# Moving four 20-byte tiles in a fused attention and feed-forward kernel, so that every large tile starts at another byte of SBUF

## The chip, the cores and the metric

The kernel runs on one core of a Trainium2 chip. The metric is the device time of one execution in microseconds (us), lower is better. Times of a kernel are given as the median of several runs; a profile is one more execution with the hardware profiler on.

## The reference

For 8 batches of 8 heads (sequence 576, head dimension 64) the program computes attention with a mask in blocks of 64, and passes the joined heads, as 4608 tokens of width 512, through a feed-forward layer with a hidden width of 2048. All in float32.

```
scores = scale * np.matmul(q, k.transpose(0, 1, 3, 2))
mask = block_i >= block_j                       # blocks of 64
scores = np.where(mask, scores, -1000000000.0)
scores = scores - np.max(scores, axis=-1, keepdims=True)
attn = np.exp(scores)
attn = attn / (np.sum(attn, axis=-1, keepdims=True) + 1e-09)
attn_out = np.matmul(attn, v)
...
x = attn_out.transpose(0, 2, 1, 3).reshape(B * S, H * D)
h = x @ w_in
g = np.maximum(0.01 * h, h)
return (g @ w_out)
```

## The kernel before

**Number format.** Where float32 products are wanted at the rate of one pass, a value is held as two tiles of type float32r, a rounded upper part and the rest: `wih` and `wil` for w_in, `woh` and `wol` for w_out, `xh` and `xl` for the tokens, `gh` and `gl` for the hidden values, `qs`, `kh`, `kl`, `vs`, `pth`, `ptl` in the attention. A product is three matmuls: upper by upper, upper by rest, rest by upper.

**Stages.** At the start the weights come in by pieces through `raw` and `val` and are split into the four weight tiles, while TensorE (PE) works at the attention of the first heads. After that each head (56 of them in the split format, `kind == "full"`) runs scores (L487), a row maximum on VectorE (DVE, `nm`, L505), the exponential on ScalarE (ACT, L514), reciprocals (`rec`, L528 and L529), normalising on whichever of GpSimd (POOL), DVE and ACT is free (L542 to L544), a transposition through DVE and a DRAM tile (`turn`, `way`, `ptm`), the product with v (L641) and the placing into `xr`, which holds one batch of tokens. Of tiles with two buffers, head i uses number i % 2: `qs0`/`qs1`, `kh0`/`kh1`, `kl0`/`kl1`, `nm0`/`nm1`, `rec0`/`rec1`.

**Feed-forward.** Tokens are taken in 18 chunks of 256. For each chunk and each of 8 pairs of hidden tiles, L805 runs two times 12 matmuls of 256 columns (weights `wih`/`wil` loaded, `xh`/`xl` streamed) into `p_h`; ACT makes `g` (L812), a cast makes `gh` (L243), a subtraction makes `gl` (L253 on DVE or L254 on POOL), and L824 runs two times 6 matmuls of 512 columns (`gh`/`gl` loaded, `woh`/`wol` streamed) into `p_o`. In all that is 3456 matmuls at L805 and 1728 at L824. The feed-forward matmuls of one batch are spread between the heads of later ones; the last chunks run alone at the end.

**Order.** The class `Plan` simulates the engines with fixed costs, once, when the program is built, and writes every engine's instructions in the order that it finds. It knows nothing of addresses, so the order doesn't depend on where a tile lies.

**Addresses.** All tiles named here come from one pool, `const`, by the helper `fixed`, and lie in a partition of SBUF one behind the other in the order in which `fixed` is called, each rounded up to 32 bytes. The first 384 bytes are taken by the program itself. A tile `nm0` of 5 float32 values so takes 32 bytes, and the pairs `nm`, `sums` and `rec` take 64 bytes each. All the large tiles have sizes that are multiples of 256 bytes, and most of 512, so that the position of one within a line of 512 bytes is handed on to those behind it. Tiles of the later pools (`raw`, `val`, `xr1`, `ptl`, `ptm`, `turn`, `v_stage` and others) begin behind the last tile of `const`.

Of the kernel before, what the change touches and what calls it, by code (L numbers as in the profile page):

```python
# [9 lines left out]
F32 = mybir.dt.float32  # L10
# [7 lines left out]
P = 128  # L18
# [3 lines left out]
NT = 5  # L22
# [204 lines left out]
def attention_ffn(ctx: ExitStack, tc: tile.TileContext, qk: bass.AP, v: bass.AP, w_in: bass.AP, w_out: bass.AP, out: bass.AP):  # L227
# [33 lines left out]
    def fixed(shape, dt, name, n=None, pool=const):  # L261
        if n is None:
            return pool.tile(shape, dt, name=name)
        return [pool.tile(shape, dt, name=f"{name}{i}") for i in range(n)]
# [3 lines left out]
    def identity(pool):  # L268
        one = fixed([P, P], F32, "ident", None, pool)
        make_identity(nc, one)  # L270
        return one

    wih = fixed([P, ND, DFF], F32R, "wih")
    wil = fixed([P, ND, DFF], F32R, "wil")
    woh = fixed([P, NF, DM], F32R, "woh")
# [24 lines left out]
    kh = fixed([P, S], F32R, "kh", 2)  # L300
    kl = fixed([P, S], F32R, "kl", 2)
    vs = fixed([P, NT, 2 * D], F32R, "vs")
    nm = fixed([P, NT], F32, "nm", 2)
    sums = fixed([P, NT], F32, "sums", 2)
    rec = fixed([P, NT], F32, "rec", 2)
    for y in range(2):
        nc.gpsimd.memset(sums[y], 1.0)
    xr = [fixed([P, ND, S], F32, "xr0"), None]
# [10 lines left out]
    xh = fixed([P, ND, CH], F32R, "xh")  # L319
    xl = fixed([P, ND, CH], F32R, "xl")  # L320
    ob = fixed([P, DM], F32, "ob")

    stage = ExitStack()
    pool = stage.enter_context(tc.tile_pool(name="wst", bufs=1, reuse_waits="tile"))
# [587 lines left out]
```

## Time and profile before

| | us |
|---|---|
| three runs: lowest, median, highest | 1120.43, 1120.84, 1126.4 |
| the profiled execution | 1119.52 |
| its span, first to last instruction | 1117.7 |
| PE busy | 1083.7 (97%) |
| DVE busy | 762.2 (68%) |
| ACT busy | 708.3 (63%) |
| POOL busy | 475.5 (43%) |

Instructions are named by the line of the kernel that issued them; L243, L244, L246, L253 and L254 belong to helpers (`copying`, `subtracting`) and stand for many tiles. PE's matmuls are pipelined: the duration of one contains some 0.16 us in which the next already streams, so that the distance between two starts tells what a matmul costs, and its duration doesn't. PEld is the loading of weights, which runs beside the matmul before.

### The profile page before, as it was taken

How to read it: one execution, taken by the hardware profiler on the slowest of the kernel's cores; microseconds unless marked ns; L12 is line 12 of the kernel's file. 1: busy time of each engine (PE TensorE's matmuls, PEld its weight loads, DVE VectorE, ACT ScalarE, POOL GpSimd, SP SyncE). 2: the span in 40 equal slices, each digit the busy share in tenths (PEclk: the TensorE clock that was granted, in tenths of full speed). 3: DMA queues.
4: the chain of work that ended last, by engine and by line, in shares of the span. 5: the costliest groups of instructions: out<-in, count | busy, mean ns of one | idle time of the engine just before them, and what ended most of it. 6: DMA issues, size and time to landing. Idle time of an engine off the chain costs nothing.

```text
span 1117.7 us, 20595 instructions
## 1 busy us (share of the span) xinstructions
PE 1083.7 (97%) x6896; PEld 971.3 (87%) x6896; DVE 762.2 (68%) x2115; ACT 708.3 (63%) x1696; POOL 475.5 (43%) x501
## 2 busy tenths in 40 slices
PE   5799999999999999999999999999999999999998
PEld 4578788888889989999999998999989998999997
DVE  6998978879878777877666678787877776400000
ACT  7998767767777766655655566676677765322222
POOL 3444244545544444433443345455444445422221
PEclk9999999999999999999999999999999999999999
DMA  7766421157766656564445456656676655200000
GB/s 235 231 201 198 133 95 61 61 173 208 199 198 189 201 170 201 176 170 147 128 151 148 128 171 185 203 171 203 176 205 185 194 156 160 59 20 19 1 20 19
DMA packets 96810, 166.24 MB, mean 149 GB/s; under 512 B 10176, under 2 KB 79808, under 8 KB 96704
## 3 DMA queue, kind: packets, MB, share of 16 engines
q1 hardware_dynamic: 96704, 164.93, 50.0%
q8 instruction: 54, 0.88, 0.3%
q14 instruction: 52, 0.43, 0.1%
HBM read 111.41 MB, written 53.48 MB: 148 GB/s over the span
## 4 chain that ended last, share of the span: by engine, by line
PE 69%; DVE 16%; ACT 6%; DMA 4%; issue 2%; SPq 1%; POOL 0%; ACTq 0%; DVEq 0%; POOLq 0%
PE p_h L805 27%; PE p_o L824 27%; PE p_t L641 6%; PE p_s L487 6%; DVE nm L505 4%; ACT prow L514 4%; DVE turn L703 2%; DVE qs L464 2%; DMA way<-turn 2%; DMA ptm<-way 2%; PE p_t L568 2%; PE p_s L481 1%; DVE p_s L498 1%; DVE ptl L253 1%; SPq L720 1%
## 5 line engine op out<-in xcount | busy, mean ns | idle before, releaser
L805 PE MATMUL p_h<-xh,wih 128*128 128x256 f32 x1152 | 327.0, 284 | 1.6 <-DVE xh L244 1.6
L805 PE MATMUL p_h<-xl,wih 128*128 128x256 f32 x1152 | 323.1, 280 | 1.0 <-DVE xl L253 0.9
L805 PE MATMUL p_h<-xh,wil 128*128 128x256 f32 x1152 | 322.5, 280 | 0.0
L254 POOL TENSOR_TENSOR gl<-g,gh 128x512 fp32r<-128x512 f32 x110 | 149.4, 1359 | 368.2 <-ACT gh L243 317.7
L805 PEld LDWEIGHTS p_h<-xl,wih 128*128 128x128 f32 x1152 | 218.6, 190 | 11.6 <-DVE xl L253 1.4
L805 PEld LDWEIGHTS p_h<-xh,wih 128*128 128x128 f32 x1152 | 217.9, 189 | 11.8 <-DVE xh L244 1.8
L805 PEld LDWEIGHTS p_h<-xh,wil 128*128 128x128 f32 x1152 | 219.4, 190 | 0.0
L514 ACT ACTIVATE prow<-p_s,nm 128x192 f32<-128x192 f32 (+4 forms) x308 | 160.0, 525 | 74.1 <-DVE nm L505 73.4
L812 ACT ACTIVATE g<-p_h 128x512 f32<-128x512 f32 x144 | 86.0, 597 | 174.6 <-PE p_h L805 168.4
L824 PE MATMUL p_o<-woh,gh 128*128 128x512 f32 x576 | 183.1, 399 | 0.0
L824 PE MATMUL p_o<-wol,gh 128*128 128x512 f32 x576 | 179.7, 393 | 0.0
L824 PE MATMUL p_o<-woh,gl 128*128 128x512 f32 x576 | 179.1, 392 | 0.0
L703 DVE STREAM_TRANSPOSE turn<-prow 128x384 f32<-128x384 f32 (+3 forms) x384 | 143.9, 401 | 33.2 <-POOL prow L542 24.0
L542 POOL TENSOR_SCALAR prow<-prow,rec 128x320 f32<-128x320 f32 (+4 forms) x142 | 77.3, 557 | 148.7 <-DVE rec L529 106.7
L505 DVE TENSOR_REDUCE nm<-p_s 128x1 f32<-128x192 f32 (+4 forms) x308 | 137.4, 480 | 3.3
L824 PEld LDWEIGHTS p_o<-woh,gl 128*128 128x128 f32 x576 | 108.2, 188 | 24.8
L824 PEld LDWEIGHTS p_o<-wol,gh 128*128 128x128 f32 x576 | 108.2, 188 | 24.4
L544 ACT ACTIVATE prow<-prow,rec 128x192 f32<-128x192 f32 (+4 forms) x124 | 75.5, 614 | 48.6 <-DVE rec L529 48.4
L243 ACT CAST gh<-g 128x512 fp32r<-128x512 f32 x139 | 86.1, 620 | 22.0 <-PE p_o L824 20.5
L254 POOL TENSOR_TENSOR ptl<-ptm,pth 128x448 fp32r<-128x448 f32 x83 | 97.6, 1193 | 3.6 <-ACT pth L243 3.6
L243 ACT CAST pth<-ptm 128x448 fp32r<-128x448 f32 x191 | 94.4, 564 | 5.4 <-DMA ptm<-way 4.9
L824 PEld LDWEIGHTS p_o<-woh,gh 128*128 128x128 f32 x576 | 90.9, 188 | 3.6 <-issue 0.4
(81 smaller groups left out, 1655.0 us busy)
## 6 DMA issues: line engine op xcount, KB each, us to landing
way<-turn SPq DMA_DIRECT2D x192, 224.0 KB, 3.0
ptm<-way SPq DMA_DIRECT2D x192, 224.0 KB, 4.3
qk_in<-in_qk SPq DMA_DIRECT2D x56, 576.0 KB, 3.8
v_stage<-in_v SPq DMA_DIRECT2D x56, 160.0 KB, 2.3
out<-ob SPq DMA_DIRECT2D x35, 256.0 KB, 2.5
raw<-in_w_in SPq DMA_DIRECT2D x32, 256.0 KB, 3.3
raw<-in_w_out SPq DMA_DIRECT2D x32, 256.0 KB, 3.4
qk_in<-in_qk SPq DMA_DIRECT2D x8, 320.0 KB, 3.6
```

The source lines that it names most:

```text
L243: one = lambda: nc.scalar.copy(dst(), src())
L254: ("POOL", pool2(n), lambda: nc.gpsimd.tensor_sub(dst(), one(), two())),
L487: go = lambda ap=ap, cols=cols, kk=kk, k0=k0, k1=k1, first=first, last=last: nc.tensor.matmul(ap, qs[z][:, cols], kk[:, k0:k1], start=firs ...
L505: [("DVE", dve(kw[t]), lambda t=t, ap=ap, flat=flat: nc.vector.tensor_reduce(nm[z][: qn[t], t : t + 1], ap[: qn[t]], axis=AX.X if flat els ...
L514: nc.scalar.activation(o, ap[: qn[t]], AF.Exp, bias=nm[z][: qn[t], t : t + 1], scale=1.0, accum_out=sums[z][: qn[t], t : t + 1])
L542: ("POOL", pool1(kw[t]), lambda: nc.gpsimd.tensor_scalar(p(), p(), by, 1.0, op0=ALU.mult, op1=ALU.mult)),
L544: ("ACT", act(kw[t], True), lambda: nc.scalar.mul(p(), p(), by)),
L641: nc.tensor.matmul(to, vs[:, j, :], src, start=start, stop=stop)
L703: nc.vector.transpose(dst, src.rearrange("p (s b i) -> p s b i", b=4, i=32))
L805: nc.tensor.matmul(hh[:, i, :], w[:, d, f * P : (f + 1) * P], x[:, d, :], start=k == 0, stop=k == len(terms) - 1)
L812: add([("ACT", act(512), lambda: nc.scalar.activation(g, hh, AF.Prelu, alpha=0.01))], rank, [("h", z)], ["g"])
L824: nc.tensor.matmul(p_o[m], a[:, i, m * P : (m + 1) * P], w[:, 2 * u + i, :], start=u == 0 and k == 0, stop=u == NU - 1 and k == 5,)
```

## The change

The two maxima tiles `nm` are allocated first in the pool, ahead of the weights, and the two reciprocal tiles `rec` last, behind the output buffer `ob`. Nothing else is edited, and the list of instructions, their order on every engine and the semaphores that they wait for are the same in both programs. What differs are start addresses in SBUF:

| tiles, in the order of the pool | before: byte in the partition, and in its 512-byte line | after |
|---|---|---|
| `wih` | 384, 384 | 448, 448 |
| `wil`, `woh`, `wol`, `pth`, `prow0_*`, `qk_in0` | at 384 of a line | at 448 |
| `qs0`, `kh0`, `kl0`, `vs` | at 384 | at 448 |
| `qs1`, `kh1`, `kl1` | at 128 | at 192 |
| `nm0`, `nm1` | 167296, 167328 | 384, 416 |
| `sums0`, `sums1` | 167360, 167392 | the same |
| `rec0`, `rec1` | 167424, 167456 | 197120, 197152 |
| `xr0`, `g`, `gh0`, `gh1`, `gl0`, `gl1`, `xh`, `xl`, `ob` | at 64 | at 0 |
| all later pools | at 64 or 320 | the same |

So the tiles from the weights to `vs` move up by 64 bytes, those from `xr0` to `ob` move down by 64, and between a weight tile of the feed-forward and the activations that it meets the distance grows by 128 bytes. No address in PSUM and none of the DRAM tiles changes.

```
@@ -270,6 +270,7 @@
         make_identity(nc, one)
         return one
 
+    nm = fixed([P, NT], F32, "nm", 2)
     wih = fixed([P, ND, DFF], F32R, "wih")
     wil = fixed([P, ND, DFF], F32R, "wil")
     woh = fixed([P, NF, DM], F32R, "woh")
@@ -300,9 +301,7 @@
     kh = fixed([P, S], F32R, "kh", 2)
     kl = fixed([P, S], F32R, "kl", 2)
     vs = fixed([P, NT, 2 * D], F32R, "vs")
-    nm = fixed([P, NT], F32, "nm", 2)
     sums = fixed([P, NT], F32, "sums", 2)
-    rec = fixed([P, NT], F32, "rec", 2)
     for y in range(2):
         nc.gpsimd.memset(sums[y], 1.0)
     xr = [fixed([P, ND, S], F32, "xr0"), None]
@@ -319,6 +318,7 @@
     xh = fixed([P, ND, CH], F32R, "xh")
     xl = fixed([P, ND, CH], F32R, "xl")
     ob = fixed([P, DM], F32, "ob")
+    rec = fixed([P, NT], F32, "rec", 2)
 
     stage = ExitStack()
     pool = stage.enter_context(tc.tile_pool(name="wst", bufs=1, reuse_waits="tile"))
```

More of the change, by code (lines that the diff above doesn't have):

```diff
@@ L271, in identity @@
         return one
+    nm = fixed([P, NT], F32, "nm", 2)
     wih = fixed([P, ND, DFF], F32R, "wih")
@@ L302, in attention_ffn @@
     vs = fixed([P, NT, 2 * D], F32R, "vs")
-    nm = fixed([P, NT], F32, "nm", 2)
     sums = fixed([P, NT], F32, "sums", 2)
-    rec = fixed([P, NT], F32, "rec", 2)
     for y in range(2):
@@ L321, in attention_ffn @@
     ob = fixed([P, DM], F32, "ob")
+    rec = fixed([P, NT], F32, "rec", 2)
     stage = ExitStack()
```

## The prediction

> **What bounds the kernel now.** I read the table of windows first, cut where the kind of work changes, then PE's own list of waits, then the chain of work that ended last.
>
> The windows of the whole core:
>
> ```profile
> core 0: us, PE busy (x) PEld busy (x) DVE busy (x) ACT busy (x) POOL busy (x), PEclk, DMA share, GB/s
> 0.00:120.00 120.00, 100.87 (x562) 78.38 (x563) 103.61 (x334) 103.48 (x295) 48.32 (x73) 1.00 0.70 214
> 120.00:300.00 180.00, 170.34 (x1094) 151.72 (x1093) 151.59 (x401) 130.23 (x327) 88.28 (x103) 0.98 0.42 126
> 300.00:976.00 676.00, 674.60 (x4357) 616.39 (x4356) 501.11 (x1373) 440.24 (x1019) 306.58 (x301) 1.00 0.59 171
> 976.00:1117.70 141.70, 137.94 (x889) 124.82 (x887) 5.88 (x10) 34.31 (x57) 32.32 (x25) 1.00 0.04 16
> ```
>
> From 300 us PE is busy 674.60 of 676 us, and in the last stretch until its final matmul: 72% of the span belongs to PE alone. DVE has 501 us there and ACT 440, so they may be late without PE noticing. PE's waits in 300:1117 confirm it; the list has one row:
>
> ```profile
> PE p_s L487 <- ACT prow L514: 1.6, 6, 0.4
> ```
>
> Before 300 us the limits are mixed: no engine is full, and the first piece of the chain is a load. So the question is almost only what a matmul at L805 or L824 costs, since these are three quarters of PE's rows. The chain shows that, by the length of unbroken runs (start, length, what):
>
> ```profile
> 470.06 4.16 PE p_o L824 x18
> 476.12 4.24 PE p_h L805 x36
> 753.15 5.65 PE p_h L805 x48
> 978.85 5.46 PE p_h L805 x48
> 1018.80 2.75 PE p_o L824 x12
> 1107.07 6.88 PE p_o L824 x30
> ```
>
> The reader should see two speeds of one and the same work, both at a granted clock of 1.00: 48 matmuls at L805 took 5.65 us (117.7 ns each) at 753 us and 5.46 us (113.75 ns each) at 979 us. L824 has 229.2 and 229.3 ns in the last two rows, 231.1 in the first. No wait stands inside these runs. The two speeds even alternate within a few rows; starts of 12 matmuls at L805 in the last stage:
>
> ```profile
> 1042.06 0.28 PE L805 MATMUL p_h<-xh,wih 128*128 128x256 f32 x1
> 1042.18 0.28 PE L805 MATMUL p_h<-xl,wih 128*128 128x256 f32 x1
> ...
> 1042.65 0.28 PE L805 MATMUL p_h<-xh,wil 128*128 128x256 f32 x1
> 1042.77 0.28 PE L805 MATMUL p_h<-xh,wih 128*128 128x256 f32 x1
> ...
> 1043.45 0.62 PE L824 MATMUL p_o<-woh,gh 128*128 128x512 f32 x2
> ```
>
> Five take 0.59 us (118 ns each), the next seven 0.80 us (114 ns). Something that the profile doesn't name makes a matmul 4 ns dearer for some rows and then lets go. This is the only place where an address could act on the time, and it's what my uncertainty hangs on.
>
> **The change part by part.** It adds, removes and reorders no instruction on any engine, and no wait differs. The four moved tiles are 20 bytes each; `nm` and `rec` are read and written by the same instructions as before. So there is no term for an operation; there are only durations that might depend on a start address. I look for each kind of user at rows of this trace in which the address already differs and all else is equal.
>
> *ACT and DVE.* Even heads use `kh0` and `qs0` (byte 384 of a 512-byte line), odd heads `kh1` and `qs1` (byte 128). ACT's cast for one odd head (window 580:600) and for the even head before it (560:580):
>
> ```profile
> L243 ACT CAST kh<-qk_in 128x576 fp32r<-128x576 f32 x1 | 0.7, 665 | 0.0
> ...
> L243 ACT CAST kh<-qk_in 128x576 fp32r<-128x576 f32 x1 | 0.7, 663 | 0.0
> ```
>
> 665 against 663 ns. A shift of 256 bytes is worth 2 ns, and a shift of 64 bytes has no reason to be worth more. With the 1700 rows at ACT and 2100 at DVE that the windows count, 2 ns each would be 3.4 and 4.2 us of busy time, nearly all under PE's cover after 300 us; uncovered, in the first 300 us with some 620 and 735 rows, it would be at most 1.5 us. I take 0.
>
> *PE in the attention.* L628 streams `ptf` (byte 64) while it loads `vf0` (byte 64) for even heads and `vf1` (byte 320) for odd ones, so that the distance between what is loaded and what is streamed differs by 256 bytes. The odd head at 87.6 us and the even one at 98.0 us:
>
> ```profile
> L628 PE MATMUL p_t<-ptf,vf 128*64 128x256 f32 x6 | 1.5, 388 | 0.0
> L628 PE MATMUL p_t<-ptf,vf 128*64 128x64 f32 x2 | 0.3, 220 | 0.0
> ...
> L628 PE MATMUL p_t<-ptf,vf 128*64 128x256 f32 x6 | 1.5, 388 | 0.0
> L628 PE MATMUL p_t<-ptf,vf 128*64 128x64 f32 x2 | 0.3, 220 | 0.0
> ```
>
> The rows are the same to the nanosecond. L487, which has the split format of the feed-forward, loads `qs` and streams `kh`; an even head (window 687.0:688.2, both tiles at 384) and an odd one (702.1:703.3, both at 128):
>
> ```profile
> L487 PE MATMUL p_s<-kh,qs 128*128 128x320 f32 x1 | 0.4, 391 | 0.0
> L487 PE MATMUL p_s<-kh,qs 128*128 128x448 f32 x1 | 0.4, 362 | 0.0
> ...
> L487 PE MATMUL p_s<-kh,qs 128*128 128x320 f32 x1 | 0.4, 389 | 0.0
> L487 PE MATMUL p_s<-kh,qs 128*128 128x448 f32 x1 | 0.4, 363 | 0.0
> ```
>
> 753 against 752 ns for the two. I take 0 for all matmuls of the attention.
>
> *PE in the feed-forward.* Here the trace has one placement only: activations at 64, weights at 384. The nearest rows are those above, which say 0. They don't cover one thing: a long run of equal matmuls in which loading and streaming repeat at a fixed distance, where the 4 ns appear. The bounds are the two speeds themselves, and I work them out under the rivals. I take 0.
>
> *DMAs.* Destinations or sources that move are `qk_in0` (576 KB at each of 56 heads), `ob`, and `g` for the last store. Their rows:
>
> ```profile
> qk_in<-in_qk SPq DMA_DIRECT2D x56, 576.0 KB, 3.8
> out<-ob SPq DMA_DIRECT2D x35, 256.0 KB, 2.5
> out<-g SPq DMA_DIRECT2D x1, 256.0 KB, 2.0
> ...
> 3.20 5.71 DMA qk_in<-in_qk
> ```
>
> No engine waits for `qk_in` behind 300 us, and `ob` is drained under matmuls. Uncovered are only the opening load, 5.71 us on the chain, and the last store, 2.0 us. If each changed by a tenth it would be 0.6 and 0.2 us; I take 0. The Trainium skill (DMA: Bandwidth & Descriptors, "How a descriptor splits into AXI transactions") says that a piece that doesn't start at a multiple of 256 bytes begins at the boundary below and pays for the bytes ahead. By it a row of the last store (2048 bytes, from byte 64 to byte 0) falls from 9 transactions to 8, an estimate of 0.2 us less, and a row of `qk_in0` keeps its number; no run shows it so far.
>
> **The sum:** 0 on every term, so 1119.5 us, the profiled execution's own time (span 1117.7 and 1.8 around it). That lies 1.3 us under the median of the runs, 1120.84, whose highest is 1126.4.
>
> The page that speaks most plainly here is SBUF — State Buffer of the Trainium skill ("Who interferes with whom"): contention comes only from the port pair that VectorE and GpSimd share, and "PE and ACT never wait on anyone." By it the sum is 0 too. But by it the two speeds of L805 should not exist either, and they do (117.7 and 113.75 ns); so I don't let that rule shut out the next two cases.
>
> **The rivals.**
>
> *A, the feed-forward matmuls all run at the higher speed.* Mechanism: loading and streaming read SBUF at once, 128 bytes further apart than before, and no longer hinder each other. For it: the slow rows come and go in the same place of each unit, with nothing waited for. Against: L628 and L487 show nothing of the kind. Price: in the last stage the chain is L805 for 50.8% of 131 us, which is 115.5 ns for each of 576:
>
> ```profile
> by line: PE p_h L805 50.8%; PE p_o L824 49.2%; PE p_t L641 0.1%
> 976.00:1107.00 131.00, 73.38 (x576) 72.81 (x576) 1.00 0.03 13
> 300.00:976.00 676.00, 294.52 (x2280) 291.20 (x2280) 1.00 0.59 171
> ...
> L805 PE MATMUL p_h<-xl,wih 128*128 128x256 f32 x192 | 53.4, 278 | 0.0
> ...
> L805 PE MATMUL p_h<-xl,wih 128*128 128x256 f32 x760 | 212.2, 279 | 0.0
> ```
>
> The last two rows are one of the three forms of L805 in the last stage (278 ns) and in 300:976 (279 ns); over the three the mean rises by 1.3 ns, so 116.8 ns for 2280. At 113.75 throughout that is 2280 x 3.05 + 576 x 1.75 = 8.0 us less. L824 from the 231.1 of the row at 470 us to the 229.2 of the one at 1019 us, for its 1141 in the middle: 2.2 us less. Together 10.2 us: **1109**.
>
> *B, they all run at the lower speed.* The same place, the other sign: the new distance makes loading and streaming meet in every row. L805 at 117.7: 2280 x 0.9 + 576 x 2.2 = 3.3 us more. For L824 the slowest pairs of the trace give 235 ns (two in 0.47 us):
>
> ```profile
> 500.24 0.63 PE L824 MATMUL p_o<-woh,gh 128*128 128x512 f32 x2
> 500.71 0.63 PE L824 MATMUL p_o<-wol,gh 128*128 128x512 f32 x2
> ```
>
> That is 1141 x 3.8 + 312 x 5.8 = 6.1 us more. Together 9.4 us: **1129**. It decides once L805's long runs in the middle are all at 117 ns and L824 leaves 231; from some 6 us (0.5%) on it can be told from no change.
>
> *C, the addresses don't move as said.* In the built programs they do; no chance.
>
> **How the numbers follow.** No change 0.43, A 0.34, B 0.23. A gets more than B since most of the long runs are at the lower speed now and so have further to fall than to rise. A measurement of this kernel tells about 0.5%, 5.6 us, from no change; the case of no change has 1114 to 1125 as its own range. Faster by over 0.5%: 0.34, within: 0.43, slower: 0.23. The range over all three is 1105 to 1130, from somewhat below A to B.
>
> **What would show it.** If I'm right, the chain of the changed kernel shows L805 runs of 48 at both 5.46 and 5.65 us, L824 at 229 to 231 ns, and the window 300:976 holds the same rows. If A is right, no L805 run stands above 114 ns, the means of L805 in 300:976 fall by 2 to 3 ns, and the last stage is shorter by 1 us. If B is right, the 24 and 48 long runs are at 117 to 118 ns and L824's means of 391 to 396 ns rise by 4 or more. If the time moves and these rows don't, my reading of what bounds the kernel is wrong, and the first 300 us must be looked at: the opening load, and DVE and ACT there.

## The result and the profile after

| | before | after |
|---|---|---|
| median of 12 runs, us | 1120.88 | 1128.74 |
| ratio after to before | | 1.007 (interval 1.005 to 1.009) |
| span of the profiled execution, us | 1117.7 | 1129.1 |
| PE busy, us | 1083.7 | 1095.5 |

The changed kernel is slower by some 8 us. The forecast was no change, 1119.5 us; the measured time is that of rival B, 1129. Among the 12 runs of the kernel before is one of 1326.78 us, which the ratio leaves out.

The windows of the changed kernel, cut as before (the last one ends with its span):

```profile
core 0: us, PE busy (x) PEld busy (x) DVE busy (x) ACT busy (x) POOL busy (x), PEclk, DMA share, GB/s
0.00:120.00 120.00, 101.10 (x553) 78.41 (x554) 102.00 (x328) 101.98 (x290) 48.75 (x73) 0.99 0.68 214
120.00:300.00 180.00, 170.37 (x1088) 151.49 (x1087) 151.03 (x404) 129.70 (x323) 87.66 (x102) 0.98 0.41 125
300.00:976.00 676.00, 674.70 (x4315) 612.79 (x4315) 501.36 (x1373) 439.62 (x1022) 304.26 (x300) 1.00 0.59 171
976.00:1129.00 153.00, 149.33 (x946) 133.77 (x944) 7.62 (x13) 37.01 (x62) 33.74 (x26) 1.00 0.04 15
```

In 300:976 PE is as full as before (674.70 of 676 us) and got through 4315 matmuls there instead of 4357. DVE, ACT and POOL are within a few us of what they were. PE's only wait in that part of the program is again one row of 1.0 us. So nothing new is waited for there: matmuls got dearer. The chain of the changed kernel, for one earlier run and then for the same runs that the prediction showed:

```profile
356.32 4.22 PE p_o L824 x18
473.99 4.22 PE p_o L824 x18
480.15 4.24 PE p_h L805 x36
760.17 5.45 PE p_h L805 x48
987.49 5.65 PE p_h L805 x48
1031.10 2.82 PE p_h L805 x24
1118.33 7.02 PE p_o L824 x30
```

The first of these in the kernel before:

```profile
353.15 4.17 PE p_o L824 x18
```

Two readings. First, the starts: in the kernel before, the others began at 470.06, 753.15, 978.85 and 1107.07 us. So the changed kernel is 3.2 us late at 353 us, 3.9 us late at the 18 matmuls of L824 at 470 us, then 7.0, 8.6 and 11.3 us late. Between the first and the last of these runs, with the same matmuls in between, it loses 8.1 us (762.01 us for 753.92). That loss grows with the feed-forward's work and belongs to no one place. Second, the lengths: L824 has 234.0 ns a matmul at the end, where it had 229.3, and the 48 at L805 that open the last stage take 5.65 us, where they took 5.46. But the 48 at L805 in the middle went the other way, from 5.65 to 5.45 us. So it isn't simply that L805 is slow at the new place.

One unit of the feed-forward (twelve matmuls at L805 and six at L824) in the last stage of the changed kernel, by its starts (start, duration), and then the end of the unit of the kernel before that the prediction showed from 1042.06 us:

```profile
1052.05 0.28 PE L805 MATMUL p_h<-xh,wih 128*128 128x256 f32 x1
...
1053.46 0.63 PE L824 MATMUL p_o<-woh,gh 128*128 128x512 f32 x2
...
1054.86 0.28 PE L805 MATMUL p_h<-xh,wih 128*128 128x256 f32 x1
```

```profile
1044.82 0.28 PE L805 MATMUL p_h<-xh,wih 128*128 128x256 f32 x1
```

A unit takes 2.81 us here (1.41 for twelve at L805, 1.40 for six at L824). Before it was 2.76, from 1042.06 to 1044.82. By single nanoseconds all such units of the last stage have 2760 before and 2813 or 2814 after. From the run of 48 at 979 us to the last 30 matmuls there are 48 units; at 53 ns they make 2.5 us, and the kernel falls back by 2.6 us in that stretch (from 8.6 to 11.3). In the middle the loss of a unit is smaller, 4.7 us on 144 units between 470 and 979 us, 33 ns each, since there part of the kernel before's units ran slowly already: of its 85 units between 300 and 976 us in which the twelve and the six follow one another directly, 34 took 2806 or 2807 ns and the others 2741 to 2760, while those of the changed kernel took 2813 to 2818.

### The profile page after: what moved, and what is told of

Read it like the earlier page. It is cut to its first block, busy times and chain, and to the rows that moved or that the text cites. A ratio compares the mean times of both kernels' runs of the same rounds, so it can differ in the third digit from the quotient of the medians.

```text
span 1129.1 us, 20595 instructions
## 1 busy us (share of the span) xinstructions
PE 1095.5 (97%) x6896; PEld 976.5 (86%) x6896; DVE 762.0 (67%) x2115; ACT 708.3 (63%) x1696; POOL 474.4 (42%) x501
## 4 chain that ended last, share of the span: by engine, by line
PE 72%; DVE 16%; ACT 6%; DMA 2%; issue 2%; SPq 1%; POOL 0%; ACTq 0%; DVEq 0%; POOLq 0%
PE p_h L805 28%; PE p_o L824 27%; PE p_t L641 6%; PE p_s L487 6%; DVE nm L505 4%; ACT prow L514 4%; DVE turn L703 3%; PE p_t L568 2%; DVE qs L464 2%; PE p_s L481 1%; PE p_t L628 1%; DMA way<-turn 1%; DVE ptl L253 1%; DVE p_s L498 1%; DVE xr L610 1%
## 5 line engine op out<-in xcount | busy, mean ns | idle before, releaser
L805 PE MATMUL p_h<-xh,wih 128*128 128x256 f32 x1152 | 326.5, 283 | 1.6 <-DVE xh L244 1.6
L805 PE MATMUL p_h<-xl,wih 128*128 128x256 f32 x1152 | 322.7, 280 | 1.0 <-DVE xl L253 0.9
L805 PE MATMUL p_h<-xh,wil 128*128 128x256 f32 x1152 | 323.1, 280 | 0.0
L805 PEld LDWEIGHTS p_h<-xl,wih 128*128 128x128 f32 x1152 | 217.6, 189 | 12.7 <-DVE xl L253 1.4
L805 PEld LDWEIGHTS p_h<-xh,wih 128*128 128x128 f32 x1152 | 217.3, 189 | 12.3 <-DVE xh L244 1.8
L805 PEld LDWEIGHTS p_h<-xh,wil 128*128 128x128 f32 x1152 | 217.5, 189 | 0.0
L824 PE MATMUL p_o<-woh,gh 128*128 128x512 f32 x576 | 184.7, 402 | 0.0
L824 PE MATMUL p_o<-woh,gl 128*128 128x512 f32 x576 | 181.1, 395 | 0.0
L824 PE MATMUL p_o<-wol,gh 128*128 128x512 f32 x576 | 181.0, 395 | 0.0
L824 PEld LDWEIGHTS p_o<-wol,gh 128*128 128x128 f32 x576 | 108.1, 188 | 26.4
L824 PEld LDWEIGHTS p_o<-woh,gl 128*128 128x128 f32 x576 | 108.1, 188 | 26.3
L824 PEld LDWEIGHTS p_o<-woh,gh 128*128 128x128 f32 x576 | 90.7, 188 | 3.8 <-issue 0.4
```

The lines of the kernel that those rows point to most:

```text
L805: nc.tensor.matmul(hh[:, i, :], w[:, d, f * P : (f + 1) * P], x[:, d, :], start=k == 0, stop=k == len(terms) - 1)
L824: nc.tensor.matmul(p_o[m], a[:, i, m * P : (m + 1) * P], w[:, 2 * u + i, :], start=u == 0 and k == 0, stop=u == NU - 1 and k == 5,)
```

## The experiments

### PE alone, 64 placements

A kernel of 16 tiles and a loop. The tiles are 4160 bytes long, so that each begins 64 bytes further in its 512-byte line than the one ahead of it: `wa` at 0, `wb` at 64, and so on.

```
...
for w in ws:
    for x in xs:
        for k in range(48):
            a, b = k % 4 * 256, k % 8 * P
            nc.tensor.matmul(p_h[:, :256], w[:, b : b + P], x[:, a : a + 256], start=k == 0, stop=k == 47)
        for k in range(24):
            a, b = k % 2 * 512, k % 8 * P
            nc.tensor.matmul(p_o, x[:, b : b + P], w[:, a : a + 512], start=k == 0, stop=k == 23)
...
```

> This kernel leaves out the whole computation but for one piece of it: PE alone, no other engine and no DMA beside it, streams and loads float32r tiles that start at each of the eight multiples of 64 bytes in a 512-byte line (wa at 0, wb at 64 ... wh at 448; xa to xh likewise). For each of the 64 pairs, 48 matmuls as at L805 (load w, stream 256 columns of x) and 24 as at L824 (load x, stream 512 columns of w). Theory D (distance): what counts is how far the streamed tile starts behind the loaded one, modulo 512 bytes; then the pairs fall in eight classes, all pairs of a class alike, and the class of the kernel before (streamed minus loaded 192 at L805, 320 at L824) is faster than that of the changed one (64 and 448): durations of about 276 to 278 ns against 281 ns at L805, 392 against 396 ns at L824. Theory W (place of one tile): rows of the table differ by where w lies (448 is bad) whatever x is, or by where x lies (0 is bad). Rival theory N: PE alone shows no difference between the pairs, all within 1 ns; then the 4 ns come from other engines' accesses beside PE.

Groups of this kernel (L38 is the first loop, L41 the second; mean ns of one is the number behind the comma):

```profile
L38 PE MATMUL p_h<-xa,wa 128*128 128x256 f32 x48 | 5.9, 283 | 0.0
L38 PE MATMUL p_h<-xb,wa 128*128 128x256 f32 x48 | 5.8, 280 | 0.0
L38 PE MATMUL p_h<-xc,wa 128*128 128x256 f32 x48 | 5.9, 282 | 0.0
L38 PE MATMUL p_h<-xd,wa 128*128 128x256 f32 x48 | 5.6, 276 | 0.0
L38 PE MATMUL p_h<-xa,we 128*128 128x256 f32 x48 | 5.9, 283 | 0.0
L41 PE MATMUL p_o<-wa,xa 128*128 128x512 f32 x24 | 5.6, 390 | 0.0
L41 PE MATMUL p_o<-wa,xb 128*128 128x512 f32 x24 | 5.8, 395 | 0.0
L41 PE MATMUL p_o<-wa,xc 128*128 128x512 f32 x24 | 5.7, 394 | 0.0
L41 PE MATMUL p_o<-wa,xd 128*128 128x512 f32 x24 | 5.7, 391 | 0.0
```

The reader should see four different numbers in the first four rows, and that `we` (256 bytes behind `wa`) gives what `wa` gives. Taken from the distances of starts behind the first 12 matmuls, all 64 pairs fall into four classes, by streamed minus loaded address modulo 256 bytes, and within a class they agree to 0.2 ns. Each run of 256 columns stands behind one of 512 here:

```
streamed minus loaded, modulo 256        0      64     128     192
256 streamed columns, as L805 (ns)   120.0   117.8   118.7   113.3
512 streamed columns, as L824 (ns)   226.7   228.6   233.0   233.4
```

Theory D holds, with a period of 256 bytes and not 512. Theory W falls: no row or column of the 8 by 8 table stands out. Theory N falls as well, since no other engine and no DMA of the kernel had work then. The kernel before has 192 at L805 and 320, which is 64, at L824; the changed one has 64 and 448, which is 192. (The activations lie behind the weights in the pool, so that their distance from the weights falls by 128 bytes with the change and doesn't grow, as was said under the change; modulo 256 the two come to the same.) Long runs at L824 should so go from 228.6 to 233.4 ns and at L805 from 113.3 to 117.8; those of the last stage went from 229.3 to 234.0 and from 113.75 to 117.7. A unit of twelve and six would lose 83 ns by these rates; it lost 53, mostly since in the kernel before L805's twelve don't run at 113.3 from the first row on (they took 1386 ns, not 1360).

### The two halves, and the same distance at other places

Only the first edit of the change (`nm` ahead of the weights):

```
+    nm = fixed([P, NT], F32, "nm", 2)
     wih = fixed([P, ND, DFF], F32R, "wih")
...
-    nm = fixed([P, NT], F32, "nm", 2)
     sums = fixed([P, NT], F32, "sums", 2)
```

> One half of the change: nm ahead of the weights, rec stays. Weights at 448 of the 512-byte line, activations at 64 as before; streamed minus loaded is 128 at L805 (192 before, 64 after). Theory D: not as after and not as before by necessity, but the same as the other half. Theory W with the weights at 448 as the cause: as after, ratio 1.007, L824 at 233 to 236 ns. Theory W with the activations at 0 as the cause: as before, ratio 1.000. Rival theory A (the attention's tiles, which move with the weights here): as after, but with L805 and L824 as before.

Only the second (`rec` last):

```
-    rec = fixed([P, NT], F32, "rec", 2)
...
     ob = fixed([P, DM], F32, "ob")
+    rec = fixed([P, NT], F32, "rec", 2)
```

> The other half: rec behind the output buffer, nm stays. Weights at 384 as before, activations at 0; streamed minus loaded is 128 at L805, as in the first half. Theory D: the same time as the first half. Theory W with the weights as the cause: as before, ratio 1.000. Theory W with the activations as the cause: as after, 1.007. Theory A: as before, since no tile of the attention but xr0 moves.

`nm` and `sums` ahead of the weights, `rec` as before:

```
+    nm = fixed([P, NT], F32, "nm", 2)
+    sums = fixed([P, NT], F32, "sums", 2)
     wih = fixed([P, ND, DFF], F32R, "wih")
...
-    nm = fixed([P, NT], F32, "nm", 2)
-    sums = fixed([P, NT], F32, "sums", 2)
     rec = fixed([P, NT], F32, "rec", 2)
```

> nm and sums ahead of the weights: weights and the attention's tiles at 0 of the line, activations at 64 as before. Streamed minus loaded is 64 at L805 and 448 at L824, the same as in the changed kernel, at other places. Theory D: as after, 1.007. Theory W: neither the weights at 448 nor the activations at 0 are there, so as before, 1.000.

`nm` ahead of the weights and 64 unused bytes ahead of `xr0`:

```
+    nm = fixed([P, NT], F32, "nm", 2)
     wih = fixed([P, ND, DFF], F32R, "wih")
...
-    nm = fixed([P, NT], F32, "nm", 2)
...
+    nc.gpsimd.memset(fixed([P, 16], F32, "gap"), 0.0)
     xr = [fixed([P, ND, S], F32, "xr0"), None]
```

> nm ahead of the weights and 64 unused bytes ahead of xr0 (with one memset of them on POOL): weights at 448 as in the changed kernel, activations at 128, so that streamed minus loaded is 192 at L805 as in the kernel before, with both at other places. What matters by the sweep is that distance modulo 256 bytes: 113.3 ns for 192, 117.7 for 64, 118.7 for 128, 120.0 for 0. So as before: ratio 0.998 to 1.002, L805 runs of the last stage at 113 to 116 ns, L824 at 229. If the place of the weights counts for itself: 1.005 to 1.009.

The last column is the time between two matmuls of L824 that are the same in all these kernels, the second of the run of 18 at 353 us and of the run of 30 at 1107 us, less that of the kernel before.

| kernel | weights, activations (512-byte line) | distance at L805, L824 (modulo 256) | ratio to before, interval | mean unit in the last stage, ns | lost from 353 us on, us |
|---|---|---|---|---|---|
| before | 384, 64 | 192, 64 | 1 | 2760 | 0 |
| after | 448, 0 | 64, 192 | 1.007 (1.005 to 1.009) | 2813 | 8.1 |
| `nm` first | 448, 64 | 128, 128 | 1.0071 (1.0054 to 1.0089) | 2824 | 10.1 |
| `rec` last | 384, 0 | 128, 128 | 1.0076 (1.0055 to 1.0097) | 2824 | 11.1 |
| `nm`, `sums` first | 0, 64 | 64, 192 | 1.0061 (1.0037 to 1.0085) | 2813 | 8.0 |
| `nm` first, gap | 448, 128 | 192, 64 | 0.9984 (0.9963 to 1.0005) | 2760 | 0.0 |

Kernels with the same distances have the same mean unit (with 128 the units vary between some 2800 and 2836 ns), wherever their tiles lie; weights at 448 are fine in the last row and bad in the second. Each half of the change alone costs as much as both. Chain rows of `nm` first, and then of `nm` first with the gap (whose lines stand one lower, L806 and L825 for L805 and L824):

```profile
987.59 5.69 PE p_h L805 x48
1118.94 7.02 PE p_o L824 x30
```

```profile
977.66 5.46 PE p_h L806 x48
1105.88 6.88 PE p_o L825 x30
```

5.69 us is 118.5 ns a matmul, the class of 128; 5.46 and 6.88 are the numbers of before to the last digit shown.

### The attention's tiles alone

`nm` between `wol` and `pth`, so that `pth` to `vs` move to the places that they have in the changed kernel, and the feed-forward's tiles don't:

```
     wol = fixed([P, NF, DM], F32R, "wol")
...
+    nm = fixed([P, NT], F32, "nm", 2)
     pth = fixed([P, turned], F32R, "pth")
...
-    nm = fixed([P, NT], F32, "nm", 2)
     sums = fixed([P, NT], F32, "sums", 2)
```

> nm between wol and pth: the tiles of the attention from pth to vs lie at 448 as in the changed kernel; the four weight tiles and all activations stay where they were before. By distance at L805 and L824 as the cause: as before, 0.998 to 1.002. If the attention's matmuls or the load of qk_in at its new place carried the loss: 1.004 to 1.009.

> The attention's tiles alone at their new place once more, with more rounds, since the first measurement (0.9976, interval 0.9954 to 0.9998) stood at the edge of a gain. If the gain is real: 0.996 to 0.999 again, with an interval that ends below 1. If it was scatter: an interval around 1. In either case the loss of the changed kernel doesn't come from these tiles.

The ratio was 0.9976 (0.9954 to 0.9998) and then, with more runs, 0.9981 (0.9963 to 1.0), with medians of 1118.44 and 1117.77 us beside 1120.05 and 1119.96 of before. So these tiles have no part in the loss. Whether there is a gain of 2 us stays at the edge of what can be told: from 353 us on both profiles of this kernel are 0.4 us ahead of the kernel before. Their first 350 us differ by 3.1 us from one execution to the other, by the start of the run of 18 at L824 that stands at 353.15 us in the kernel before:

```profile
351.28 4.16 PE p_o L824 x18
354.38 4.16 PE p_o L824 x18
```

### Behind other matmuls

Eight tiles in steps of 32 bytes with `w` at 0, as in the first sweep; and 48 matmuls as at L805 behind four of other widths (here 192):

```
...
for k in range(4):
    nc.tensor.matmul(p_t[:, :192], xs[0][:, k * P : k * P + P], xs[6][:, :192], start=k == 0, stop=k == 3)
for k in range(48):
    nc.tensor.matmul(p_h[:, :256], w[:, k % 8 * P : k % 8 * P + P], xs[6][:, k % 4 * 256 : k % 4 * 256 + 256], start=k == 0, stop=k == 47)
...
```

> This kernel leaves out the whole computation but for PE alone: first w (at 0) with eight tiles xa to xh in steps of 32 bytes (0 to 224), 48 matmuls as at L805 and 24 as at L824 for each. If the unit is 64 bytes, x at 32 is as x at 0 or 64, at 96 as at 64 or 128, and so on; if it is finer, values between. Second, 48 matmuls as at L805 at distance 192, and then at 64, each behind four matmuls of 64, 96, 128, 192, 256, 320, 384, 448 and 512 columns. If the distance alone decides, all nine rows of 192 are at 276 ns and all of 64 at 281. If the phase with which PE enters a run is kept, as the two speeds of long runs in the kernel before suggest, some rows of 192 are at 281 and some of 64 at 276.

Rows of the first part (`xb` at 32, `xf` at 160, `xg` at 192, `xh` at 224), and of the second: `xg` is distance 192, `xc` distance 64; L54, L58 and L74 stand behind widths of 128, 192 and 448, L82, L86 and L110 behind 64, 96 and 448:

```profile
L39 PE MATMUL p_h<-xb,w 128*128 128x256 f32 x48 | 5.8, 279 | 0.0
L39 PE MATMUL p_h<-xf,w 128*128 128x256 f32 x48 | 5.9, 281 | 0.0
L39 PE MATMUL p_h<-xg,w 128*128 128x256 f32 x48 | 5.6, 276 | 0.0
L39 PE MATMUL p_h<-xh,w 128*128 128x256 f32 x48 | 5.8, 281 | 0.0
...
L54 PE MATMUL p_h<-xg,w 128*128 128x256 f32 x48 | 5.7, 277 | 0.0
L58 PE MATMUL p_h<-xg,w 128*128 128x256 f32 x48 | 5.8, 281 | 0.0
L74 PE MATMUL p_h<-xg,w 128*128 128x256 f32 x48 | 5.6, 276 | 0.0
...
L82 PE MATMUL p_h<-xc,w 128*128 128x256 f32 x48 | 5.7, 278 | 0.0
L86 PE MATMUL p_h<-xc,w 128*128 128x256 f32 x48 | 5.9, 281 | 0.0
L110 PE MATMUL p_h<-xc,w 128*128 128x256 f32 x48 | 5.6, 276 | 0.0
```

At 32 bytes off the good place (`xf`, `xh`) the gain is gone, so 64 isn't the unit. And the same 48 matmuls at the same addresses run at either speed, by what stood ahead of them. By the last twelve distances of starts, all 18 rows of the second part have 113.3 or 117.8 ns, nothing between:

```
width of the four ahead   64     96    128    192    256    320    384    448    512
distance 192           113.3  113.3  113.3  117.8  117.8  117.8  117.8  113.3  113.3
distance 64            113.3  117.8  117.8  117.8  117.8  117.8  117.8  113.3  117.8
```

A run settles at one of two speeds within its first matmuls (at most five here) and keeps it to the last of the 48; the distance decides which entries lead to the fast one. The twelve of the prediction, five at 118 ns and seven at 114, show the same settling behind L824. Behind 512 columns, which is L824's width, that is so at 192 and not at 64. So a run of L805 may well go the other way, as that of 48 in the middle did, which stands behind a score (L487) and not behind L824; its own entry wasn't rebuilt.

### All units of the feed-forward

A try at a better place: `nm`, `sums` and `rec` between `wil` and `woh`, so that L805 keeps 192 and L824 gets 0, the best of the four for 512 columns:

```
     wil = fixed([P, ND, DFF], F32R, "wil")
+    nm = fixed([P, NT], F32, "nm", 2)
+    sums = fixed([P, NT], F32, "sums", 2)
+    rec = fixed([P, NT], F32, "rec", 2)
     woh = fixed([P, NF, DM], F32R, "woh")
...
-    nm = fixed([P, NT], F32, "nm", 2)
-    sums = fixed([P, NT], F32, "sums", 2)
-    rec = fixed([P, NT], F32, "rec", 2)
```

> nm, sums and rec between wil and woh: w_in's tiles (384) and the activations (64) stay, so L805 keeps its distance of 192; w_out's tiles go to 64, so that at L824 streamed minus loaded falls from 320 (64 modulo 256) to 0. The sweep has 226.6 ns for 0 and 228.6 for 64: 1728 x 2.0 = 3.5 us less, ratio 0.997. The attention's tiles move by 192 together. If L824 in the kernel isn't what it is with PE alone: 1.000. If the distance at L824 alone had spoilt the changed kernel, L805 should stay at 113 to 118 ns here.

The gain didn't come: 1.0014 (0.9993 to 1.0035), where 0.997 was expected, with a unit of 2800 ns in the last stage instead of 2760 and 3.6 us lost from 353 us on. Chain rows of this kernel:

```profile
979.46 5.66 PE p_h L805 x48
1109.62 6.84 PE p_o L824 x30
```

L824 in its long run is better (228.0 ns for 229.3), but L805 now settles at its slow speed behind it (5.66 us for 48, where it was 5.46). In the units of the last stage both parts are dearer, L805's twelve at 1413 ns for 1386 and L824's six at 1387 for 1374. The single rates of the first sweep don't add up, so a last kernel ran PE alone on eight whole units for each of 64 placements of activations `x`, of `g` and of w_out's part `w`, against w_in's part `wi`:

```
...
for u in range(8):
    for k in range(12):
        a, b = k // 3 * 256, k % 8 * P
        nc.tensor.matmul(p_h[:, :256], wi[:, b : b + P], x[:, a : a + 256], start=k == 0, stop=k == 11)
    for k in range(6):
        a, b = k % 2 * 512, k % 2 * 256 + u % 2 * P
        nc.tensor.matmul(p_o, g[:, b : b + P], w[:, a : a + 512], start=k == 0, stop=k == 5)
...
```

> PE alone again, the rest of the computation is left out: eight times the kernel's unit of 12 matmuls as at L805 and 6 as at L824, for each of 64 placements. wi lies at 0 modulo 256; xa to xd, ga to gd and wa to wd (w_out's part) at 0, 64, 128 and 192. Which of two speeds a run takes depends on how it is entered (the second sweep), so the pure rates of the first sweep can't be added up. If PE alone explains the kernel, the placement of before (xd, gd, wa) gives 2.75 to 2.76 us for a unit, as in its last stage, that of after (xb, gb, wa) 2.81, and that of nm or rec alone (xc, gc, wa) 2.82 to 2.83. The split one (xd, gd, wd) should be no better than 2.76. If there is a placement better than before's, the least that the first sweep allows is 12 x 113.3 + 6 x 226.6 = 2.72 us, some 5 us over the 144 units of the kernel.

Mean of the last four of seven distances between units (of the last three for 128, 128, 0, whose units repeat by threes), and the last-stage unit of the kernel with that placement:

```
x, g, w (bytes modulo 256 from wi)        PE alone, ns    kernel, ns
192, 192, 0     before                    2760            2760
64, 64, 0       after, nm and sums first  2814            2813
128, 128, 0     nm first, rec last        2825            2824
192, 192, 192   three tiles in between    2800            2800
64, 128, 192    best of 64                2753            -
0, 0, 64        among the worst           2840            -
```

PE alone repeats the last stage of the kernels to 2 ns. The kernel has 288 such units (the expectation counts them in pairs, so that its 5 us for the least conceivable unit should read some 11). The placement of before is 7 ns a unit behind the best of 64. That would be 2.0 us if all units ran as in the last stage, which couldn't be told from no change; in the middle, where units of before take 2741 to 2807 ns, the best placement's worth is not shown, since it wasn't built into the kernel.

## Why the prediction was wrong

**What bounds the kernel** was read rightly. From 300 us on PE alone counts, no wait changed, and the time went where the prediction said that an address could act: into L805 and L824.

**The zero at ACT, DVE and the attention** held. ACT's casts of `kh` take 662 ns in the mean of 55, before and after, with `kh0` and `kh1` moved to 448 and 192; the attention's tiles alone cost nothing.

**The DMAs** held too: `out<-ob` lands in 2.5 and `out<-g` in 2.0 us, before and after. The 0.2 us less for the last store, the estimate by the Trainium skill (DMA: Bandwidth & Descriptors, "How a descriptor splits into AXI transactions"), didn't come: at that resolution a step from 2.0 to 1.8 would have shown. The opening load lasted 6.27 us on the chain instead of 5.71, in one profiled execution of each. Its new place doesn't explain that: `nm` first has `qk_in0` at the same 448 and 5.41 us there, and the kernel with the attention's tiles alone, also at 448, has 6.08 in one execution and 5.67 in the other.

**The zero at PE in the feed-forward is the step that failed**, at "The nearest rows are those above, which say 0". Both rows were blind. `vf0` and `vf1` lie 1280 bytes apart, which is five full periods of 256, so that L628 compared a distance with itself. `qs` and `kh` both move by the same number of bytes from even to odd heads, so that their distance doesn't change at all. A natural experiment that shifts by the period, or shifts both operands alike, shows no difference whatever the mechanism costs. The prediction named the gap (a long run at a fixed distance) and gave the two speeds as bounds, and then let the blind rows decide. The term measured 8.1 us between the runs at 353 and 1107 us, beside 7.9 us between the medians of the two kernels. By the distances of starts, 4.3 us of it are L824's, 3.5 us L805's and 0.4 us all other matmuls'. The 3.2 us of lateness ahead of 353 us in the profiled executions can't be told from scatter, since two executions of one kernel differ by 3.1 us there.

**Rival B** had the place and the sign and nearly the size: L805 at 117.7 ns was forecast for it and 117.5 came (24 in 2.82 us); L824 was taken from its slowest pairs as 235 ns and came to 234.0 in the last run. That 1129 us meets 1128.74 so closely is in part luck: it was 9.4 us on top of an execution 1.4 us under the median, and 7.9 came. Two of its signs failed. The 48 matmuls in the middle were to be at 117 to 118 ns and ran at 113.5; the second sweep shows that the speed also hangs on the entry. L824's mean durations were to rise by 4 ns or more, and rose by 2 to 3 (from 396, 393 and 392 to 399, 395 and 395 in 300:976). **Rival A**'s argument, that most long runs were slow already and had further to fall, treated the two speeds as a draw; but they follow from address and entry, and of four distances at L805 the kernel before had the one that runs at 113.3 ns behind 512 columns. That a change away from a good place can mostly lose was not weighed.

**The rule of the Trainium skill** (SBUF — State Buffer, "Who interferes with whom") that PE never waits on anyone would have made the sum 0. Against it stand 113.3 to 120.0 ns for one matmul with nothing at work but PE: the measurement decides. In that sweep the distance between what PE loads and what it streams counts, and neither address alone. That the two reads hinder each other is the nearest explanation, but no run took one of them away.

## What to carry to other kernels

The distance between the start of what the matmuls stream and of what they load was worth up to 6% of a float32r matmul of 256 columns here (113.3 to 120.0 ns). So where PE is full, a tile added or dropped ahead in a pool can move the time of a kernel with no instruction changed, by 0.7% in this one. Before an edit of tiles is judged, compare these addresses modulo 256; padding that kept the distance kept the time (the row with the gap). Before a row of the trace is taken as a natural experiment, ask by how much it shifts what is asked about, and whether that is a multiple of a possible period.

## What the runs showed of the hardware

- A float32r matmul of 128 loaded and 256 streamed columns, in a long run with PE alone behind matmuls of 512 columns, costs 113.3, 117.8, 118.7 or 120.0 ns, by streamed minus loaded address of 192, 64, 128 or 0 modulo 256 bytes; one of 512 streamed columns, behind matmuls of 256, costs 226.7 to 233.4 ns. Steps of 32 bytes give other values still (116.7 ns at 32, 118.3 at 224).
- At one address pair two speeds are possible, 113.3 and 117.8 ns (seen at distances 192 and 64), and a run keeps for 48 matmuls the one at which it settles in its first few. What is inside PE or SBUF that holds it there stays open: the runs show that it hangs on address modulo 256 and on the width of the matmuls ahead, and that no other engine is needed for it.
- PE alone on a copy of the unit gives the unit time of the kernel's last stage to 2 ns in 2800, in all four placements that both were run with.
